# Seven block products instead of eight for the last product of attention and a bilinear FFN

## The chip, the cores and the metric

The kernel runs on one core of a Trainium2 chip. The metric is the time of one execution on the device in microseconds, the median of several runs. The profile is that of one execution, recorded on the chip. PE is the matmul engine, PEld its weight loads, DVE the vector engine, ACT the scalar engine, POOL GpSimd, SP the engine whose queue issues the transfers.

## The reference

```python
# attention over 32 memory slots: batch 8, 8 heads, 576 tokens, head_dim 64
a = softmax(phi, axis=2)                       # over tokens
k_m = einsum('bhsm,bhsd->bhmd', a, k); v_m = einsum('bhsm,bhsd->bhmd', a, v)
attn = softmax(q @ k_m.T / 8, axis=-1)         # 576 tokens x 32 slots
x = attn @ v_m                                 # heads side by side: 4608 tokens x 512
# bilinear FFN
g = (x @ w1) * (x @ w2)                        # 4608 x 1024
out = (g @ w3) @ w_out                         # 4608 x 512
```

The kernel uses that products may be bracketed otherwise: with M = v_m times w1 (or w2), (x @ w1) is attn @ M, and with W = w3 @ w_out (1024 x 512), computed once, out = g W.

## The kernel before, in words

All matmuls that matter take their operands in two pieces: a high part rounded to the fast fp32r format and a low part, the rest (`split`: ACT casts the high part, DVE subtracts to get the low one). A product is then three matmuls: high by high, low by high, high by low.

The work goes over 8 batches. A batch has 576 tokens in two halves n of 288. Its steps have names, and three lists at the top of the program (START, FIRST for batch 0, STEADY for the others) give the order in which they are written out. PE and SP run in exactly that order. The order within DVE, ACT and POOL is set by a scheduler when the kernel is built, which simulates a timeline; each engine then runs its list in order, one instruction after the other, and waits where an input isn't ready.

- START converts the float64 weights (step C: words picked apart on ACT and DVE), computes W in two halves (W), keeps it as pieces Wh, Wl (K), and prepares the attention of batch 0.
- A (`ab_unit`, 16 for each batch, one for each half n and each of eight f blocks of 128): two groups of six matmuls of 128x288, a = attn·M1 and b = attn·M2, into two PSUM banks. ACT copies a to SBUF, DVE multiplies it with b to g, and the split gives gh and gl.
- O (`out_part`, 16 for each batch: 2 halves n, 4 blocks o of 128 output features, 2 parts): 12 matmuls of 128x288, W's pieces by gh and gl, added up in one PSUM bank over both parts. ACT copies the result to osb and SP sends it out, 144 KB each, eight for a batch.
- The attention of the next batch lies between: `top`, `exp`, `norm` (softmax of phi, tile ph, among the A's), `turn`, `mem`, `blocks` (memories km, vm), and, among the O's, `sc` (scores), `se`, `sn` (softmax of the scores), `pr` (probabilities at, split to ah and al) and four M (`memory_weights`, split to mh and ml). `kv2`, `q2` and `phi2` are loads, issued by SP among its outputs.

PSUM has eight banks: a and b twice each, o twice, and a pair x.

Of the kernel before, what the change touches and what calls it, by code (L numbers as in the profile page):

```python
# [8 lines left out]
F32 = mybir.dt.float32  # L9
# [26 lines left out]
def memory_attention__then__bilinear_ffn_kernel(  # L36
# [39 lines left out]
    ps_o = ctx.enter_context(tc.tile_pool(name="ps_o", bufs=2, space=bass.MemoryType.PSUM))  # L76
    ps_x = ctx.enter_context(tc.tile_pool(name="ps_x", bufs=1, space=bass.MemoryType.PSUM))
# [73 lines left out]
    def attention(b):  # L151
# [22 lines left out]
        def turn(i):  # L174
            ps = psum_pair().rearrange("p k (c t x) -> p (k c) t x", c=2, t=NT)
# [40 lines left out]
        def blocks():  # L216
            ps = psum_pair()[:, 0, : NT * P]
# [7 lines left out]
        def scores(n, banks):  # L225
# [5 lines left out]
            ps = [x[:, :HALF] for x in banks()]  # L231
# [30 lines left out]
        def probs(n):  # L262
            if n == 0:
                v["at"] = att.tile([P, 2, S], F32, name="at", tag="ph")
                ah = att.tile([P, 2, S], F32R, name="ah", bufs=2)
                al = att.tile([P, 2, S], F32R, name="al", tag="al", bufs=2)
                ready["A", b] = (ah, al)
            ah, al = ready["A", b]
            nc.vector.transpose(out=v["at"][:, n], in_=v["s"][:, n].rearrange("p k m -> p (k m)"))
            split(ah[:, n], al[:, n], v["at"][:, n])  # L270

        steps = {"top": top, "exp": exp, "norm": norm, "mem": memories, "blocks": blocks}
        steps |= {f"turn{i}": lambda i=i: turn(i) for i in (0, 4)}
        for n in range(2):
            steps |= {f"sc{n}": lambda n=n: scores(n, pair), f"sc{n}p": lambda n=n: scores(n, banks_ab)}
# [7 lines left out]
    def memory_weights(b):  # L283
# [3 lines left out]
        def step(q, banks):  # L287
            one = None if banks else psum_pair()
            ps = banks() if banks else [one[:, t] for t in range(NT)]
            for g in range(NG):  # L290
                for t in range(NT):
                    d = slice((1 - t) * D, (2 - t) * D)
                    nc.tensor.matmul(  # L293
                        ps[t][g * M : (g + 1) * M],
# [7 lines left out]
            if banks:  # L302
                for t in range(NT):
                    split(mh[:, t], ml[:, t], ps[t].rearrange("p (w f) -> p w f", w=2))
            else:
                split(mh, ml, one.rearrange("p t (w f) -> p t w f", w=2))
# [20 lines left out]
    init = None  # L327
# [17 lines left out]
    def convert(i):  # L345
# [11 lines left out]
        if i < FIRST_LATE:  # L357
            u = init.tile([P, CW], I32, name="u", bufs=2)
# [190 lines left out]
```

## Time and profile before

| what | value |
|---|---|
| runs | 554.55, 555.44, 554.29 us; median 554.55 |
| profiled execution, span | 554.0 us |
| the median less the span | 0.55 us |
| a steady batch, from its first O to that of the next | 59.63 us |
| busy in one steady batch: PE, DVE, ACT, POOL | 59.63, 32.30, 25.13, 0.00 us |
| matmuls | 4696 |

The profile gives busy times by engine and groups of instructions by line, operation and tile; after the bar of a group stand the busy time, the mean duration in ns, and the idle time of the engine just before with what ended it. The chain is the work that ended last, followed backwards. In the timeline a row is start, duration, engine, line, operation, and in brackets the wait before it. Line numbers before and after the change differ: the split is L111/L112 before and L102/L103 after, and L495/L496 are the new splits of the block factors.

### The profile page before, as it was taken

The page shows a single profiled execution, that of the slowest core. Times are in us where ns is not written, and L with a number is a line of the kernel's source. Part 1 is how long each engine was busy: PE and PEld are TensorE (multiplying, and loading weights), DVE is VectorE, ACT ScalarE, POOL GpSimd, SP SyncE. Part 2 cuts the span into 40 slices and gives each one's busy share as a digit, 9 for nine tenths or more (in the row PEclk, how much of TensorE's full clock was granted, in tenths as well). Part 3 has the DMA queues.
Part 4 walks back from the last instruction along what each step waited for, and adds up shares of the span by engine and source line. Part 5 has one row for each costly group of instructions (what it writes and reads, how often), then busy time and mean ns, then how long its engine had stood idle before and what let it go on. Part 6 is the DMA issues. An engine that isn't in the chain of part 4 may idle for free.

```text
span 554.0 us, 11182 instructions
## 1 busy us (share of the span) xinstructions
PE 538.2 (97%) x4696; PEld 470.1 (85%) x4696; DVE 311.4 (56%) x599; ACT 253.7 (46%) x522; POOL 0.7 (0%) x6
## 2 busy tenths in 40 slices
PE   3999989999999999999999999999999999999997
PEld 1453458988999899989998899989998999899997
DVE  5887997637457624681558335762478155824500
ACT  5877784624544434452543444333544354424411
POOL 0000000000000000000000000000000000000000
PEclk9999999999999999999999999999999999999999
DMA  8999628008140511333043304050123200110011
GB/s 316 407 372 391 254 76 297 4 24 300 64 158 27 168 37 38 136 118 95 4 172 99 96 22 164 22 170 33 70 104 128 87 2 2 34 44 11 1 44 44
DMA packets 28819, 64.17 MB, mean 116 GB/s; under 512 B 2144, under 2 KB 10336, under 8 KB 28768
## 3 DMA queue, kind: packets, MB, share of 16 engines
q1 hardware_dynamic: 28768, 63.45, 32.7%
q8 instruction: 37, 0.61, 0.5%
q14 instruction: 14, 0.11, 0.1%
HBM read 54.00 MB, written 9.44 MB: 115 GB/s over the span
## 4 chain that ended last, share of the span: by engine, by line
PE 91%; DVE 4%; DMA 2%; ACT 1%; issue 1%; DVEq 0%; ACTq 0%
PE o L465 37%; PE a L440 18%; PE b L440 18%; PE x L194 3%; PE a L387 2%; PE b L387 2%; PE a L293 2%; PE x L293 2%; DMA raw<-in_w_out 1%; PE x L180 1%; PE b L293 1%; PE x L234 1%; DVE w L377 1%; DMA raw<-in_w3T 1%; DVE w L376 1%; PE o L387 1%
## 5 line engine op out<-in xcount | busy, mean ns | idle before, releaser
L465 PE MATMUL o<-gh,Wh 128*128 128x288 f32 x512 | 152.9, 299 | 0.0
L465 PE MATMUL o<-gl,Wh 128*128 128x288 f32 x512 | 151.1, 295 | 0.0
L465 PE MATMUL o<-gh,Wl 128*128 128x288 f32 x512 | 151.1, 295 | 0.0
L465 PEld LDWEIGHTS o<-gh,Wh 128*128 128x128 f32 x512 | 96.8, 189 | 11.9 <-issue 11.9
L451 DVE TENSOR_TENSOR gr<-b,a_sb 128x288 f32<-128x288 f32 x128 | 58.5, 457 | 84.2 <-PE b L440 80.9
L111 ACT CAST gh<-gr 128x288 fp32r<-128x288 f32 x128 | 55.4, 433 | 99.4 <-DVE gr L451 99.4
L465 PEld LDWEIGHTS o<-gl,Wh 128*128 128x128 f32 x512 | 96.3, 188 | 0.0
L465 PEld LDWEIGHTS o<-gh,Wl 128*128 128x128 f32 x512 | 96.2, 188 | 0.0
L112 DVE TENSOR_TENSOR gl<-gr,gh 128x288 fp32r<-128x288 f32 x128 | 58.5, 457 | 56.7 <-ACT gh L111 56.4
L440 PE MATMUL b<-ah,mh 128*128 128x288 f32 x256 | 75.6, 295 | 2.7 <-DVE Wl L112 2.7
L440 PE MATMUL a<-ah,mh 128*128 128x288 f32 x256 | 78.0, 305 | 0.0
L440 PE MATMUL a<-al,mh 128*128 128x288 f32 x256 | 75.9, 296 | 0.0
L440 PE MATMUL b<-al,mh 128*128 128x288 f32 x256 | 75.9, 296 | 0.0
L440 PE MATMUL b<-ah,ml 128*128 128x288 f32 x256 | 75.9, 296 | 0.0
L440 PE MATMUL a<-ah,ml 128*128 128x288 f32 x256 | 75.8, 296 | 0.0
L470 ACT COPY osb<-o 128x288 f32<-128x288 f32 x64 | 25.3, 395 | 82.8 <-PE o L465 71.5
L449 ACT COPY a_sb<-a 128x288 f32<-128x288 f32 x128 | 50.5, 394 | 8.0 <-PE a L440 7.4
L440 PEld LDWEIGHTS a<-ah,mh 128*128 128x128 f32 x256 | 48.4, 189 | 4.2 <-issue 2.0
L440 PEld LDWEIGHTS b<-ah,mh 128*128 128x128 f32 x256 | 48.4, 189 | 3.0 <-DVE Wl L112 3.0
L440 PEld LDWEIGHTS b<-ah,ml 128*128 128x128 f32 x256 | 48.5, 189 | 0.0
L440 PEld LDWEIGHTS a<-ah,ml 128*128 128x128 f32 x256 | 48.5, 189 | 0.0
L440 PEld LDWEIGHTS b<-al,mh 128*128 128x128 f32 x256 | 48.4, 189 | 0.0
(89 smaller groups left out, 649.1 us busy)
## 6 DMA issues: line engine op xcount, KB each, us to landing
kv<-in_kv SPq DMA_DIRECT2D x16, 1024.0 KB, 7.8
q<-in_qT SPq DMA_DIRECT2D x8, 1152.0 KB, 6.0
outT<-osb SPq DMA_DIRECT2D x64, 144.0 KB, 1.8
raw<-in_w3T SPq DMA_DIRECT2D x7, 1024.0 KB, 11.9
ph<-in_phiT SPq DMA_DIRECT2D x8, 576.0 KB, 4.0
raw<-in_w SPq DMA_DIRECT2D x4, 1024.0 KB, 17.2
raw<-in_w_out SPq DMA_DIRECT2D x3, 1024.0 KB, 10.5
kv<-in_w SPq DMA_DIRECT2D x3, 1024.0 KB, 14.5
```

Source lines behind the costliest of these rows:

```text
L111: nc.scalar.copy(out=hi, in_=src)
L112: nc.vector.tensor_tensor(out=lo, in0=src, in1=hi.bitcast(F32), op=ALU.subtract)
L180: nc.tensor.transpose(ps[:, c, t], v["ph"][:, t, at : at + P], ident)
L194: nc.tensor.matmul(ps[h * M : (h + 1) * M, t, : 2 * D], lhsT=v["a"][:, i, t, h * M : (h + 1) * M], rhs=kvt[i][:, (4 * t + h) * 2 * D : (4 ...
L234: nc.tensor.matmul(ps[t][g * M : (g + 1) * M], lhsT=km[b % 2][t * D : (t + 1) * D, g], rhs=v["q"][t * D : (t + 1) * D, g, n * HALF : (n + ...
L293: nc.tensor.matmul(ps[t][g * M : (g + 1) * M], lhsT=vm[b % 2][d, g], rhs=w12_sb[q][d, :, g], start=True, stop=True,)
L387: nc.tensor.matmul(pw[r][i], lhsT=x[:, i * P : (i + 1) * P], rhs=wos[k // half][:, k % half], start=k == 0, stop=k == NF - 1,)
L440: nc.tensor.matmul(p, lhsT=x[:, t, w, fc : fc + P], rhs=y[:, n, t * HALF : (t + 1) * HALF], start=i == 0, stop=i == len(todo) - 1,)
L449: nc.scalar.copy(out=a_sb, in_=ps[0])
L451: nc.vector.tensor_tensor(out=gr, in0=ps[1], in1=a_sb, op=ALU.mult)
L465: nc.tensor.matmul(v["p"], lhsT=x[f // half][:, f % half, oc], rhs=y, start=f == 0 and i == 0, stop=f == NF - 1 and i == 2)
L470: nc.scalar.copy(out=osb, in_=v["p"])
```

## The change

The matrix W is cut in four blocks (f halves by feature halves), and g in four (token halves n by f halves): G00, G01 for half 0, G10, G11 for half 1. The eight block products of the four output blocks become seven, by Strassen's scheme in Winograd's form, with sums of blocks of g on one side and sums of blocks of W on the other. The products are called 1, 2, 6, 5, 7, 3, 4 in the order in which they are used, and their factors on g's side X1 = G00, X2 = G01, X6 = S2, X5 = the sum of G10 and G11, X7 = S3, X3 = S4, X4 = G11. Each product is 2 O's (two column parts j of 128) of 12 matmuls, so a batch has 14 O's.

- `ab_unit` writes g into a 128x1152 tile of its block (no split there), and POOL does the block sums: S3 (L478), the sum in place of G10 (L480), S2 (L481), each four times 128x288, and S4 once 128x1152 (L489).
- `factor` (steps X1 to X7) splits a whole block: ACT casts 128x1152 into sh (L495), DVE subtracts into sl (L496), two buffers of each.
- `out_part`: products 1, 6, 7, 4 add up in the pair of banks o, 2 alone and 5, 3 in the pair x. After 1, 6, 5 and 4 ACT copies the running sum to a tile c (128x576); after 2, 7 and 3 DVE adds the PSUM pair to a c (L540). Four outputs of 288 KB go out, after 2, 7, 3 and 4.
- `keep` makes four blocks of pieces of W from raw copies: ACT copies and casts, POOL subtracts.
- PSUM is four pairs of two banks: ab twice, o, x. An A takes one pair and a pair is free when both its banks have been read. Scores and M use pairs of ab.
- The order lists change with it. ah and al have one buffer instead of two. In STEADY the load of ph stood with eight O's behind it and stands now behind the output of product 7, with three O's behind it.

```diff
-O sc0 sc1p Mp O se0 O se1 O q2 sn0 O pr0 O sn1 O pr1 M Mp Mp O phi2 O O O O O O O O
+O sc0p sc1p X6 O O se0 O X5 M M O se1 O X7 q2 sn0 O pr0 O sn1 X3 O pr1 M M O O X4 phi2 O O O
...
-        gr = big.tile([P, HALF], F32, name="gr", bufs=2)
-        nc.vector.tensor_tensor(out=gr, in0=ps[1], in1=a_sb, op=ALU.mult)
-        gh = big.tile([P, HALF], F32R, name=f"gh{n}{f}")
-        gl = big.tile([P, HALF], F32R, name=f"gl{n}{f}")
-        split(gh, gl, gr)
-        g[n, f] = (gh, gl)
...
+        nc.vector.tensor_tensor(out=G[n, f // half][:, k], in0=both[:, 1, :HALF], in1=a_sb, op=ALU.mult)
+        G["done"].add((n, f))
+        if (1 - n, f) in G["done"]:
+            sub = nc.gpsimd.tensor_tensor
+            top, low = G[0, 0][:, k], G[1, 0][:, k]
+            if f < half:
+                sub(out=G["S3"][:, k], in0=top, in1=low, op=ALU.subtract)
+            else:
+                sub(out=low, in0=low, in1=G[1, 1][:, k], op=ALU.add)
+                G["S2"].append(lambda: sub(out=top, in0=low, in1=top, op=ALU.subtract))
+
+    def factor(i, G):
+
+        if i == 6:
+            for f in G["S2"]:
+                f()
+            x = G[0, 1]
+            G["S4"] = lambda: nc.gpsimd.tensor_tensor(out=x, in0=x, in1=G[0, 0], op=ALU.subtract)
+        if i == 3:
+            G["S4"]()
+        src = {1: G[0, 0], 2: G[0, 1], 6: G[0, 0], 5: G[1, 0], 7: G["S3"], 3: G[0, 1], 4: G[1, 1]}[i]
+        hi = big.tile([P, half, HALF], F32R, name="sh", tag="sh", bufs=2)
+        lo = big.tile([P, half, HALF], F32R, name="sl", tag="sl", bufs=2)
+        in_turn("hi", nc.scalar.copy(out=hi, in_=src))
+        in_turn("lo", nc.vector.tensor_tensor(out=lo, in0=src, in1=hi.bitcast(F32), op=ALU.subtract))
+        G["X", i] = (hi, lo)
...
+        s, oc = weights[i]
+        oc = slice(oc * OH + j * P, oc * OH + (j + 1) * P)
+        hi, lo = G["X", i]
+        for k in range(half):
+            for m, (x, y) in enumerate(((Wh, hi), (Wl, hi), (Wh, lo))):
                 nc.tensor.matmul(
+                    ps[:, j, :HALF],
+                    lhsT=x[s][:, k, oc],
+                    rhs=y[:, k],
...
+        if i in (1, 6, 5, 4):
+            c = G["C", i] = const.tile([P, 2, HALF], F32, name="c", tag=f"c{n_c[0] % 4}")
+            n_c[0] += 1
+            nc.scalar.copy(out=c, in_=ps)
+        if i in (2, 7, 3):
+            c = G["C", {2: 1, 7: 5, 3: 6}[i]]
+            nc.vector.tensor_tensor(out=c, in0=ps, in1=c, op=ALU.add)
+        if i in (2, 7, 3, 4):
+            n, oh = {2: (0, 0), 3: (0, 1), 4: (1, 0), 7: (1, 1)}[i]
+            at = b * S + n * HALF
+            dst = outT[oh * OH : (oh + 1) * OH, at : at + HALF].rearrange("(j p) s -> p j s", j=2)
+            nc.sync.dma_start(out=dst, in_=c)
```

How the instructions stand, in rows of line, operation, out<-in and size. First DVE in the O phase of a steady batch, from the sums of the score softmax on. Before:

```order
L257 TENSOR_REDUCE ss_1914<-s_sb 128x18
L258 TENSOR_SCALAR ss_1875<-ss_1875 128x18
L258 TENSOR_SCALAR ss_1914<-ss_1914 128x18
L259 RECIPROCAL ss_1875<-ss_1875 128x18
L259 RECIPROCAL ss_1914<-ss_1914 128x18
L260 TENSOR_TENSOR s_sb<-s_sb,ss_1875 128x576
L260 TENSOR_TENSOR s_sb<-s_sb,ss_1914 128x576
L269 STREAM_TRANSPOSE at<-s_sb 128x576 x2
L112 TENSOR_TENSOR al<-at,ah 128x576 x2
```

And DVE in the same place in the change (g_1285 is the tile of G10, g_1283 that of G00, s_1287 is S3):

```order
L496 TENSOR_TENSOR sl<-g_1283,sh 128x1152
L249 TENSOR_REDUCE ss_1794<-s_sb 128x18
L249 TENSOR_REDUCE ss_1832<-s_sb 128x18
L540 TENSOR_TENSOR c<-x,c 128x576
...
L496 TENSOR_TENSOR sl<-g_1285,sh 128x1152
...
L103 TENSOR_TENSOR ml_1742<-ab,mh_1741 128x1024
...
L103 TENSOR_TENSOR ml_1755<-ab,mh_1754 128x1024
L252 TENSOR_TENSOR s_sb<-s_sb,ss_1832 128x576
L261 STREAM_TRANSPOSE at<-s_sb 128x576 x2
L496 TENSOR_TENSOR sl<-s_1287,sh 128x1152
L103 TENSOR_TENSOR al<-at,ah 128x576 x2
```

X6's and X5's subtractions, the addition of product 2 and two of the ml stand now among the softmax rows, and X7's (s_1287) stands behind both transposes.

Next DVE at the end of a steady batch and the start of the next, in the change:

```order
L540 TENSOR_TENSOR c<-o,c 128x576
L496 TENSOR_TENSOR sl<-g_1286,sh 128x1152
L540 TENSOR_TENSOR c<-x,c 128x576
L149 TENSOR_REDUCE mx<-ph 128x2
L160 TENSOR_SCALAR sm<-sm 128x2
L161 RECIPROCAL sm<-sm 128x2
L472 TENSOR_TENSOR g_1956<-ab,a_sb 128x288
```

Before, the maximum of ph stood behind the last ml and ahead of the first multiplication too; the additions c<-o,c (product 7) and c<-x,c (product 3) and X4's subtraction (g_1286) are new, and the load of ph is issued by SP behind the output that the first of them fills.

Last ACT around the first A's, where the last weights are converted and the probabilities of batch 0 are split. Before:

```order
L252 ACTIVATE s_sb<-s_sb 128x576
L111 CAST mh_435<-x 128x1024
L373 ACTIVATE w_2_83<-kv_388 128x1024
L373 ACTIVATE w_3_84<-q 128x1024
L111 CAST ah<-at 128x576
L374 ACTIVATE al<-kv_376 128x1024
L111 CAST Wh_474<-o 128x512 x2
```

And in the change:

```order
L361 ACTIVATE w_2_80<-kv_393 128x1024
L361 ACTIVATE w_3_81<-q 128x1024
L362 ACTIVATE ul<-q 128x1024
L361 ACTIVATE w_3_81<-kv_553 128x1024
L102 CAST ah<-at 128x576
L408 COPY raw_489<-ab 128x512 x2
L408 COPY raw_756<-o 128x512 x2
L389 CAST Wh_483<-raw_489 128x512 x2
L389 CAST Wh_483<-raw_756 128x512
```

Two more conversion rows stand ahead of the first ah, the last of them of the tile kv_553 that is loaded last, and raw copies stand ahead of the casts of W.

More of the change, by code (lines that the diff above doesn't have):

```diff
@@ L214, in memories, with blocks @@
                 )
[L216 to L217 removed]
+        def blocks(bank):
+            ps = bank()[:, 0, : NT * P]
             for t in range(NT):
@@ L223, in blocks, with scores @@
                 nc.vector.tensor_copy(out=vm[b % 2][vo : vo + D], in_=p4[vo : vo + D, t])
-        def scores(n, banks):
+        def scores(n, bank):
             if n == 0:
@@ L230, in scores @@
                 v["s"] = s_sb[:, : NT * S].rearrange("p (n k m) -> p n k m", n=2, m=M)
-            ps = [x[:, :HALF] for x in banks()]
+            both = bank()
+            ps = [both[:, t, :HALF] for t in range(NT)]
             for g in range(NG):
@@ L270, in probs @@
             split(ah[:, n], al[:, n], v["at"][:, n])
[L272 to L275, printed above, removed]
+        steps = {"top": top, "exp": exp, "norm": norm}
+        for x, bank in (("", pair_x), ("p", pair_ab)):
+            steps |= {f"turn{i}{x}": lambda i=i, bank=bank: turn(i, bank) for i in (0, 4)}
+            steps |= {f"mem{x}": lambda bank=bank: memories(bank), f"blocks{x}": lambda bank=bank: blocks(bank)}
+            steps |= {f"sc{n}{x}": lambda n=n, bank=bank: scores(n, bank) for n in range(2)}
         for name, f in (("se", soft_exp), ("sn", soft_norm), ("pr", probs)):
@@ L285, in memory_weights, with step @@
         ms = ready["M", b] = []
-        def step(q, banks):
-            one = None if banks else psum_pair()
-            ps = banks() if banks else [one[:, t] for t in range(NT)]
+        def step(q, bank):
+            ps = bank()
             for g in range(NG):
@@ L301, in step @@
             ml = const.tile([P, NT, 2, FQ], F32R, name=f"ml{q}", tag=f"m{m_tags[2 * q + 1]}")
[L302 to L306, printed above, removed]
+            split(mh, ml, ps.rearrange("p t (w f) -> p t w f", w=2))
             ms.append((mh, ml))
-        return [lambda banks=None, q=q: step(q, banks) for q in range(NQ)]
+        return [lambda bank, q=q: step(q, bank) for q in range(NQ)]
     def rows(w, k, n):
@@ L424, in memory_attention__then__bilinear_ffn_kernel, with ab_unit @@
                 steps[what]()
-    big = ctx.enter_context(tc.tile_pool(name="big", bufs=1))
-    def ab_unit(b, n, f, g):
+    last = len(START) - START[::-1].index("C")
+    with tc.tile_pool(name="init", bufs=1) as init:
+        for i in range(BUFS):
+            fetch(i)
+        start(START[:last])
+    big = ctx.enter_context(tc.tile_pool(name="big", bufs=1, reuse_waits="tile"))
+    start(START[last:])
+    def ab_unit(b, n, f, G):
         ah, al = ready["A", b]
@@ L432, in ab_unit @@
         fc = f * P % FQ
-        ps = []
-        for w, name in enumerate("ab"):
-            p = psum(ps_ab, name)[:, :HALF]
+        both = pair_ab()
+        for w in range(2):
             todo = []
```

160 lines of the change are left out of this document (96 added, 64 removed).

## The prediction

> **What bounds the kernel now.** I read the page's busy shares first, then the chain that ended last, then a table of stretches.
>
> ```profile
> PE 538.2 (97%) x4696; PEld 470.1 (85%) x4696; DVE 311.4 (56%) x599; ACT 253.7 (46%) x522; POOL 0.7 (0%) x6
> PE 91%; DVE 4%; DMA 2%; ACT 1%; issue 1%; DVEq 0%; ACTq 0%
> ```
>
> PE is busy for 97% of the span and 91% of the chain, but a busy share says nothing of where spare time lies. The table of stretches (span, then busy time of PE, PEld, DVE, ACT, POOL; clock; DMA share; GB/s) does, for one steady batch (start of one O phase to the next) and for the last O phase:
>
> ```profile
> 230.93:290.56 59.63, 59.63 (x574) 55.60 (x573) 32.30 (x66) 25.13 (x59) 0.00 (x0) 1.00 0.27 90
> 525.39:554.00 28.61, 25.46 (x192) 25.22 (x191) 0.92 (x2) 3.63 (x9) 0.00 (x0) 1.00 0.13 43
> ```
>
> In a steady batch PE has no gap in 59.63 us, at full clock. A matmul taken away is therefore time taken away, and any PE wait that appears is time added. The price of a matmul comes from the last O phase in the chain (start, us, what); the 295 to 299 ns that groups show are modelled ends which overlap.
>
> ```profile
> 108.59 1.59 PE o L465 x12
> ...
> 244.22 1.02 PE x L293 x16
> 246.96 14.52 PE o L465 x108
> ...
> 525.39 25.47 PE o L465 x192
> ```
>
> 25.47 / 192 = 0.1327 us for one matmul, 12 × 0.1327 = 1.59 us for one O.
>
> **1. Matmuls removed.** 14 O's instead of 16 in a batch, 24 matmuls fewer: 24 × 0.1327 × 8 = **-25.4 us**, all of it on the path.
>
> **2. The seventh product's low factor (X7).** The splits that stood in the A phase (one gh and gl for each A) become one cast and one subtraction of 128x1152 for each product, and four of the seven now run in the O phase, in DVE's queue among the next batch's softmax. What DVE did there before, and when:
>
> ```profile
> 230.77 0.29 PE L465 MATMUL o<-gh,Wh 128*128 128x288 f32 x1
> 233.28 0.85 DVE L243 STREAM_TRANSPOSE s_sb<-x 128x288 f32<-128x288 f32 x2 [0.82 <-PE x L234]
> 235.59 0.72 DVE L251 TENSOR_TENSOR s_sb<-s_sb,st 128x576 f32<-128x576 f32 x1
> 236.22 0.74 DVE L250 TENSOR_REDUCE st<-s_sb 128x18 f32<-128x576 f32 x1
> 241.91 1.43 DVE L269 STREAM_TRANSPOSE at<-s_sb 128x576 f32<-128x576 f32 x2
> 243.43 1.43 DVE L112 TENSOR_TENSOR al<-at,ah 128x576 fp32r<-128x576 f32 x2
> 253.62 1.35 DVE L158 TENSOR_REDUCE mx<-ph 128x2 f32<-128x1152 f32 x1 [3.61 <-DMA ph<-in_phiT]
> 263.18 0.46 DVE L451 TENSOR_TENSOR gr<-b,a_sb 128x288 f32<-128x288 f32 x1 [6.09 <-PE b L440]
> ```
>
> T is the first matmul of the O phase, 230.77. From T+2.5 the first four rows of DVE run back to back, and the two "at" transposes end at 243.34, T+12.6. DVE takes rows in order, and in the change X7's subtraction stands behind those transposes. Prices by size:
>
> ```profile
> L112 DVE TENSOR_TENSOR gl<-gr,gh 128x288 fp32r<-128x288 f32 x128 | 58.5, 457 | 56.7 <-ACT gh L111 56.4
> L112 DVE TENSOR_TENSOR al<-at,ah 128x576 fp32r<-128x576 f32 x16 | 11.5, 755 | 0.6
> L112 DVE TENSOR_TENSOR ml<-x,mh 128x1024 fp32r<-128x1024 f32 x11 | 13.5, 1225 | 9.2 <-ACT mh L111 9.2
> L111 ACT CAST gh<-gr 128x288 fp32r<-128x288 f32 x128 | 55.4, 433 | 99.4 <-DVE gr L451 99.4
> L111 ACT CAST ah<-at 128x576 fp32r<-128x576 f32 x16 | 10.7, 675 | 22.3 <-DVE at L269 22.3
> ```
>
> The step from 288 to 576 elements is 298 ns, so 1152 cost 755 + 2 × 298 = 1351 ns on DVE, and 675 + 2 × 242 = 1159 ns on ACT. Rows that follow each other on DVE start some 0.09 us sooner than their durations add up to (235.59 to 236.22 is 0.63 for a row of 0.72), so each is taken at 0.09 less, except the last. Now ahead of X7's subtraction and not there before: those of X6 and X5 (2 × 1.27), the addition after product 2 (128x576, taken as the 755 row: 0.66), and two ml of 128x1024 (2 × 1.14) where there was one in two halves of 0.6 (+1.1). T+12.6 + 2.5 + 0.7 + 1.1 + 1.35 = T+18.2. PE comes to the third matmul of product 7's first O, the first to read the low factor, after 8 O's (12.7), two scores (about 1.2 with their joints), two M (1.9 for both; the chain has 1.02 for one) and two matmuls (0.26): T+16.0. **It waits 2.2 us.** The cover is those 16 us; no other work of PE stands ahead. What is late next is X3's subtraction, one O later; it follows "al" on DVE by then in time. In six steady batches 6 × 2.2 = **+13.2**, in batch 0, whose queue is alike, **+2.5**. Bounds: if DVE's starts keep no order of mine and X7 slips ahead, 0; if ACT's casts hold DVE up by one cast, 3.4 each.
>
> Before product 6 the block sums on POOL have to be done. POOL computes nothing in the rows of before but these:
>
> ```profile
> masks.py:199 POOL TENSOR_SCALAR_AFFINE_SELECT ident<-ident 128x128 f32<-128x128 f32 x1 | 0.3, 292 | 0.1
> L536 POOL MEMSET const-bfloat16-1.0<- 128x1 bf16 x1 | 0.1, 102 | 0.0
> ```
>
> Estimates from them: in proportion to 128 elements in 292 ns, 288 cost 0.66 us and 1152 cost 2.6; at DVE's rate 0.46 and 1.35. I take the POOL row's. Then S2's last piece is there by about T+3.7, the cast and subtraction of X6 need 2.5 more, DVE's queue comes to it by T+7.9, and PE asks for it at T+9.7 (4 O's, the scores, two M); S4 of 2.6 us has until product 3. So the sums cost **nothing** at either bound: the 32 us of O phase hide them. Twice that price (1.3 a piece) would still reach X6 in time. For splits in the A phase (X1, X2) DVE has room, since its 128 gl rows of 0.46 us are gone.
>
> **3. The next batch's ph.** Its load is issued by SP, in order, behind the outputs. Before:
>
> ```profile
> 249.68 0.39 SPq L119 DMA_DIRECT2D ph<-in_phiT  x1
> ph<-in_phiT SPq DMA_DIRECT2D x8, 576.0 KB, 4.0
> L164 ACT ACTIVATE ph<-ph,mx 128x576 f32<-128x576 f32 x16 | 12.3, 770 | 18.7 <-DVE mx L158 18.7
> ```
>
> It went out at T+18.9, and the first multiplication of the next A's came at 263.18, after DVE had idled 6.09 us: well hidden. Now it stands behind the output of product 7, whose addition runs at about T+25 (12 O's and the stall), so it goes out at T+25.5, lands 4.0 later, and the maximum (1.35) and two exponentials (0.77 each, behind the copy of product 4 on ACT), then two small rows, come ahead of A's first multiplication in DVE's queue: T+33.2 to 33.7. A's third unit needs the pair of banks that this multiplication frees at T+32.7. I take **0.8 us in each of six batches, +4.8**; the bounds are 0 (it lands 1 us sooner) and 1.5.
>
> **4. Batch 0 and the start-up.** Rows of ACT, SP, DVE and PE around the first A's:
>
> ```profile
> 70.43 0.67 ACT L111 CAST ah<-at 128x576 fp32r<-128x576 f32 x1 [2.55 <-DVE at L269]
> 78.96 1.13 ACT L373 ACTIVATE w<-kv 128x1024 f32<-128x1024 f32 x1 [0.20 <-DMA kv<-in_w]
> 73.30 0.54 SPq L343 DMA_DIRECT2D kv<-in_w  x1
> 98.41 1.34 DVE L158 TENSOR_REDUCE mx<-ph 128x2 f32<-128x1152 f32 x1
> 75.13 0.40 PE L440 MATMUL a<-ah,mh 128*128 128x288 f32 x1
> 80.51 0.40 PE L440 MATMUL b<-ah,mh 128*128 128x288 f32 x1 [2.73 <-DVE Wl L112]
> 81.54 0.44 PE L440 MATMUL a<-al,mh 128*128 128x288 f32 x1
> 81.78 0.44 PE L440 MATMUL a<-ah,ml 128*128 128x288 f32 x1
> ```
>
> A conversion that waits for a load (issue to landing about 5.5 us, 73.30 to 78.8) now stands on ACT ahead of the first "ah", so that the second matmul of the first A starts near 77.8 instead of 75.4; behind it ACT now copies four products raw and casts both these and their sums where it had one cast for each, and the third A starts near 84.2 instead of 81.4. Then ph is asked for about 1 us later and X1's split and the maximum stand ahead of a multiplication. I carry **+5.3** to the first O; 3 if only the first wait stays, 8 if the W pieces on POOL (11264 elements a partition, 25 us in proportion to its row) hold ACT's casts up. In batch 0 the memories' blocks are followed by the scores with no O between, **+1.2** for DVE's four small copies.
>
> **5. The end.** The last matmul is followed by a copy and an output, now twice as large:
>
> ```profile
> 550.93 0.40 ACT L470 COPY osb<-o 128x288 f32<-128x288 f32 x1 [2.49 <-PE o L465]
> outT<-osb SPq DMA_DIRECT2D x64, 144.0 KB, 1.8
> ```
>
> +0.24 for the copy (433 to 675 ns is that step) and about +0.35 for twice the bytes (ph's 576 KB take 2.2 us more than 144): **+0.6**.
>
> **The sum** against the span of 554.0: -25.4 + 13.2 + 2.5 + 4.8 + 5.3 + 1.2 + 0.6 = +2.2, 556.2. The median of the runs, 554.55, lies 0.55 above the span; with it 556.8, and I say **557**. A steady batch is about as long as before: 59.63 - 3.18 + 2.2 + 0.8 = 59.45.
>
> **Rivals.**
>
> R1, POOL stops DVE. S4 (2.6 us, about T+3.7 to T+6.2) lies over DVE's first softmax subtraction, due at 235.59, T+4.8. If an instruction of DVE that reads two SBUF tiles stands until POOL's is over, the whole queue ahead of X7 moves by 1.4 us: 7 × 1.4, and about 1 us at X6 or X3 of the last batch: 557 + 11 = **568**. Against it: POOL's column is 0.00 in every steady stretch, so no run here shows either answer. That rule is in the Trainium skill, page "SBUF — State Buffer", section "Who interferes with whom": a DVE instruction with two SBUF inputs contends with a GpSimd instruction that reads SBUF, and the later one blocks fully.
>
> R2, X7 is not late. If DVE has the subtraction by T+16.0, 2.2 us sooner than I add up (rows that need less than I took, or a PE that comes later), the stalls of part 2 go and the change gains: 557 - 15.7 = **541**. For it: DVE is busy 32.30 of 59.63 us. Against it: the rows ahead stand in one queue and ran back to back before.
>
> R3, the waits cost PE its clock. After the gap of 2.73 us before 80.51, matmuls went 0.24 us apart (81.54 to 81.78) for some 2.5 us, about 1.1 us lost. If each wait of 2.2 us does it too, 7 × 1.1 and one at the start-up: **566**. For it: 2.2 us is close to 2.73. Against it: it is shorter, and the steady row, with its short joints at scores and M, has a clock of 1.00, so no row shows where between the two it turns.
>
> **How the numbers follow.** Forecast 0.40 (its own range 552 to 563: stalls of 1.5 to 3 us at X7), R1 0.30, R2 0.20, R3 0.10. About 0.2%, 1.1 us, is what a measurement can tell here. Faster: R2 and 0.04 of the forecast's low end, 0.24; same: 0.10 of the forecast, which lies just above; slower: the rest, 0.66. Half of R2 below 540 and the upper parts of R1 and R3 above 571 are left out, so the range is 540 to 571.
>
> **What would show it.** A PE wait of about 2 us for DVE's L496 at product 7's third matmul in batches 0 to 6, and none at the others (part 2); a DVE queue with no gaps ahead of it. A PE wait under 1.5 us at the third A of batches 1 to 6, ended by DVE's multiplication behind the maximum (part 3). The first O some 5 us later than 108.59 bears out part 4. R1 shows as a softmax subtraction of over 2 us on DVE while POOL runs L489; R2 as a PE with no gap in the O phase; R3 as a granted clock under 1.00 there. I am wrong at the root if PE waits for POOL (L481, L489) or for a bank.

## The result: 7% slower

The changed kernel takes 594.92 us (median of 592.76 to 595.85) against 555.00 for the kernel before (554.29 to 556.27), a ratio of 1.0705 [1.0676, 1.0733]. The forecast was 557, with a range of 540 to 571: the side came as forecast, the size did not. The profiled execution has a span of 593.8 us, 39.8 more than before.

Busy shares, and the granted clock in 40 slices, from the page of the changed kernel:

```profile
PE 540.2 (91%) x4504; PEld 452.1 (76%) x4504; DVE 354.0 (60%) x522; ACT 269.9 (45%) x413; POOL 134.0 (23%) x142
PEclk9998988999999989997999899999999799989999
PE 53%; DVE 27%; ACT 7%; DMA 6%; issue 4%; POOL 3%; SPq 0%; ACTq 0%; DVEq 0%; POOLq 0%
L523 PE MATMUL o<-sl,Wh 128*128 128x288 f32 x256 | 79.9, 312 | 21.9 <-DVE sl L496 21.9
```

PE does 192 matmuls fewer and yet is not busy for less time (540.2 against 538.2). Two things are new: 27% of the chain is DVE's (4% before), and the clock has dips. The last row shows one of the places where PE waits: 21.9 us in all ahead of the first matmul that reads a low factor.

The table of stretches (span, then busy time of PE, PEld, DVE, ACT, POOL; clock; DMA share; GB/s) for the start-up, one steady batch and the last O phase of the changed kernel:

```profile
0.00:122.59 122.59, 100.31 (x517) 59.11 (x518) 81.59 (x116) 80.69 (x107) 41.71 (x46) 0.96 0.65 239
378.61:442.06 63.45, 59.70 (x549) 52.53 (x549) 37.64 (x57) 26.22 (x44) 12.35 (x13) 0.97 0.26 85
566.00:593.80 27.80, 22.44 (x168) 21.97 (x166) 12.00 (x10) 8.94 (x11) 4.30 (x3) 1.00 0.12 43
```

Where the 39.8 us come from, by the starts of the batches (first O of each), with 3.18 us (24 matmuls) taken off what each batch took before:

| stretch | before, less 3.18 a batch | after | lost |
|---|---|---|---|
| to the first O | 108.59 | 122.59 | 14.0 |
| batch 0 | 59.53 | 65.53 | 6.0 |
| five steady batches | 5 x 56.45 | 318.27 | 36.0 (7.2 each) |
| the batch ahead of the last O phase | 52.76 | 59.61 | 6.8 |
| last O phase | 25.43 | 27.80 | 2.4 |
| all, less 25.4 for the matmuls | | | 65.2 - 25.4 = 39.8 |

Inside the steady batch of the second row the 7.0 us lost are: a PE wait for X7's low factor 3.06; the pair of M behind it 3.53 us long instead of 1.88, +1.65; the scores 1.48 instead of 1.13, +0.35; the first five A's, from the first to the last of them, +0.86; and about 1 us in short joints. Its O phase, PE's waits first and then DVE and POOL (timeline of the changed kernel: start, duration, engine, line, what, and in brackets the wait before; T, its first matmul, is 378.45):

```profile
398.65 0.41 PE L523 MATMUL o<-sl,Wh 128*128 128x288 f32 x1 [3.06 <-DVE sl L496]
415.66 0.40 PE L462 MATMUL ab<-ah,mh 128*128 128x288 f32 x1 [0.57 <-DVE g L472]
...
383.26 2.78 DVE L243 TENSOR_TENSOR s_sb<-s_sb,st 128x576 f32<-128x576 f32 x1
386.74 0.76 DVE L243 TENSOR_TENSOR s_sb<-s_sb,st 128x576 f32<-128x576 f32 x1
...
395.92 1.43 DVE L261 STREAM_TRANSPOSE at<-s_sb 128x576 f32<-128x576 f32 x2
397.28 1.32 DVE L496 TENSOR_TENSOR sl<-s,sh 128x1152 fp32r<-128x1152 f32 x1
...
382.75 2.68 POOL L489 TENSOR_TENSOR g<-g,g 128x1152 f32<-128x1152 f32 x1
```

The softmax subtraction that took 0.72 before takes 2.78 here, and it lies under POOL's S4, which starts 0.51 us ahead of it and ends at 385.43. The same instruction on the other half, 0.7 us later with POOL idle, takes 0.76. Two us later than it would be, DVE comes through its queue to X7, and PE waits for it. What the wait does to PE is in the table of stretches around it (the clock is the column behind POOL):

```profile
394.00:398.00 4.00, 1.59 (x13) 1.36 (x11) 4.00 (x6) 1.27 (x3) 0.00 (x0) 1.00 0.58 219
398.00:402.00 4.00, 3.35 (x34) 1.93 (x42) 3.20 (x4) 1.65 (x3) 0.00 (x0) 0.77 0.00 0
402.00:406.00 4.00, 4.00 (x41) 2.40 (x26) 2.27 (x2) 2.56 (x3) 0.00 (x0) 0.80 0.01 4
```

0.23 and 0.20 of two times 4 us are 1.7 us, the length by which the pair of M has grown. In two of the six batches (64.68 and 64.33 us long) the clock stayed at half for some 6 us behind the same wait. So the theory that the experiments had to test: **one POOL row stops a DVE row for 2.0 us (R1), the wait at X7 grows to a length behind which PE loses its clock (R3), and each steady batch pays both, 3.5 us in this one.** The rival: X7 is late because DVE's queue is too full, whatever POOL does, and S4 is a bystander. Apart from both stands the start-up, with its own 14.0.

### The profile page after: what moved, and what is told of

It reads as the page before. It is cut to its first block, busy times and chain, and to the rows that moved or that the text cites. A ratio compares the mean times of both kernels' runs of the same rounds, so it can differ in the third digit from the quotient of the medians.

```text
span 593.8 us, 10668 instructions
## 1 busy us (share of the span) xinstructions
PE 540.2 (91%) x4504; PEld 452.1 (76%) x4504; DVE 354.0 (60%) x522; ACT 269.9 (45%) x413; POOL 134.0 (23%) x142
## 3 DMA queue, kind: packets, MB, share of 16 engines
q1 hardware_dynamic: 28256, 63.45, 30.6%
## 4 chain that ended last, share of the span: by engine, by line
PE 53%; DVE 27%; ACT 7%; DMA 6%; issue 4%; POOL 3%; SPq 0%; ACTq 0%; DVEq 0%; POOLq 0%
PE ab L462 29%; PE o L523 7%; PE ab L375 5%; DVE sl L496 5%; DMA ph<-in_phiT 4%; DVE ml L103 4%; DVE s_sb L243 3%; PE ab L285 3%; DVE s_sb L235 2%; PE x L185 2%; DVE st L242 2%; DVE ss L249 2%; ACT ph L155 2%; POOL Wl L390 2%; PE x L523 2%
## 5 line engine op out<-in xcount | busy, mean ns | idle before, releaser
L462 PE MATMUL ab<-ah,mh 128*128 128x288 f32 x512 | 156.0, 305 | 12.4 <-DVE g L472 11.8
L462 PE MATMUL ab<-al,mh 128*128 128x288 f32 x512 | 152.5, 298 | 3.3 <-DVE al L103 3.3
L462 PE MATMUL ab<-ah,ml 128*128 128x288 f32 x512 | 152.2, 297 | 0.0
L462 PEld LDWEIGHTS ab<-ah,mh 128*128 128x128 f32 x512 | 97.5, 190 | 19.9 <-DVE g L472 16.4
L462 PEld LDWEIGHTS ab<-al,mh 128*128 128x128 f32 x512 | 97.5, 190 | 3.5 <-DVE al L103 3.5
L523 PE MATMUL o<-sl,Wh 128*128 128x288 f32 x256 | 79.9, 312 | 21.9 <-DVE sl L496 21.9
L462 PEld LDWEIGHTS ab<-ah,ml 128*128 128x128 f32 x512 | 97.6, 191 | 0.0
L478 POOL TENSOR_TENSOR s<-g,g 128x288 f32<-128x288 f32 x32 | 25.8, 805 | 289.1 <-DVE g L472 289.1
L496 DVE TENSOR_TENSOR sl<-g,sh 128x1152 fp32r<-128x1152 f32 x48 | 67.9, 1415 | 28.4 <-ACT sh L495 28.4
L523 PE MATMUL o<-sh,Wh 128*128 128x288 f32 x256 | 79.3, 310 | 0.0
L523 PE MATMUL o<-sh,Wl 128*128 128x288 f32 x256 | 77.4, 302 | 0.0
L495 ACT CAST sh<-g 128x1152 fp32r<-128x1152 f32 x48 | 55.5, 1156 | 42.8 <-PE o L523 28.5
L523 PEld LDWEIGHTS o<-sh,Wh 128*128 128x128 f32 x256 | 50.0, 195 | 17.1 <-issue 12.1
```

The lines of the kernel that those rows point to most:

```text
L462: nc.tensor.matmul(both[:, w, :HALF], lhsT=x[:, t, w, fc : fc + P], rhs=y[:, n, t * HALF : (t + 1) * HALF], start=i == 0, stop=i == len(to ...
L478: sub(out=G["S3"][:, k], in0=top, in1=low, op=ALU.subtract)
L495: in_turn("hi", nc.scalar.copy(out=hi, in_=src))
L496: in_turn("lo", nc.vector.tensor_tensor(out=lo, in0=src, in1=hi.bitcast(F32), op=ALU.subtract))
L523: nc.tensor.matmul(ps[:, j, :HALF], lhsT=x[s][:, k, oc], rhs=y[:, k], start=i in (1, 2, 5) and k == 0 and m == 0, stop=k == half - 1 and m ...
```

## Experiments on the steady batch

**S4 left out** (e1_no_s4). Product 3 takes G01 in the place of S4, so S4's block sum is not computed; everything else stands.

```diff
-        if i == 3:
-            G["S4"]()
```

> S4 is left out: product 3 takes G01 itself, so the output is another one; POOL has no 128x1152 row any more, all else stands. Theory (POOL stops DVE): the first softmax subtraction, 2.7 us in a steady batch of the changed kernel, is back at 0.75, so X7's low factor comes 2.0 us sooner and PE's wait for it falls from 3.1 to about 1.1 us; if the slow clock behind that wait goes too, another 1.7 us a batch. 594.9 less 7 x 2.0, and less 1.5 in the last batch, is about 579 with the slow clock and about 568 without. Rival (the subtraction is long for a reason of its own, such as its operands or PSUM): it stays at 2.7 us and the time within 2 us of 594.9.

Measured: 570.44 us, ratio 1.0272 [1.0256, 1.0288]; 24.5 us fewer than the change, for eight POOL rows of 2.7 us, for none of which PE shows a wait. The group of the first softmax subtraction (busy us, mean ns):

```profile
L243 DVE TENSOR_TENSOR s_sb<-s_sb,st 128x576 f32<-128x576 f32 x16 | 11.8, 740 | 0.2
```

In the changed kernel some six of its sixteen rows are stretched:

```profile
L243 DVE TENSOR_TENSOR s_sb<-s_sb,st 128x576 f32<-128x576 f32 x16 | 24.2, 1515 | 0.2
```

PE at product 7 without S4 (timeline):

```profile
385.24 0.40 PE L521 MATMUL o<-sl,Wh 128*128 128x288 f32 x1 [1.25 <-DVE sl L494]
```

The stretch behind that wait and a whole steady batch without S4:

```profile
385.30:389.30 4.00, 4.00 (x47) 2.45 (x48) 2.78 (x4) 2.29 (x4) 0.00 (x0) 1.00 0.00 0
367.27:427.44 60.17, 57.79 (x549) 52.30 (x549) 35.43 (x57) 26.00 (x44) 9.66 (x12) 1.00 0.27 90
```

The wait falls from 3.06 to 1.25, and the clock behind it stays at 1.00, so both halves of the 3.5 us go together. But S4 is also work taken away; so:

**S4 kept, and put elsewhere** (e5_s4_in_A). From batch 1 on S2 and S4 are computed piece by piece among the A's, and X2, which reads the tile that S4 overwrites, is split in four pieces there. POOL does the same arithmetic as in the change.

```diff
+        if b and n == 0 and f >= half:
+            piece(k, G)                      # cast and subtraction of X2's piece k
...
-                G["S2"].append(lambda: sub(out=top, in0=low, in1=top, op=ALU.subtract))
+                S2 = lambda: sub(out=top, in0=low, in1=top, op=ALU.subtract)
+                if b:
+                    S2()
+                    x = G[0, 1][:, k]
+                    sub(out=x, in0=x, in1=top, op=ALU.subtract)
```

> S4 is kept, but from batch 1 on X2 is split in four pieces of 128x288 as its blocks of g become ready, and POOL forms S2 and S4 piece by piece among the A's; batch 0 is as it was. Theory (it is S4's place over the softmax that costs, not S4): only one piece of 0.8 us is left near the first softmax subtraction, which falls from 2.7 to under 1.6 us; the wait at product 7 falls from 3.1 to 1.3 to 2 us, the slow clock behind it goes, and the time is 569 to 578, near the run without S4 (570.4). Rival (POOL's work stops DVE wherever it stands): the same microseconds return among the A's as waits for g, 585 or more.

Measured: 569.04 us, 1.0233 [1.0210, 1.0256], as fast as without S4. L243 means 736 ns, the wait at X7 is 1.01, the scores are back at 1.13 (in the change their second pair of banks waits for a multiplication that stands on DVE behind X2's subtraction of a whole block). So it is S4's place, not its amount, that costs about 25 us (of the 26 gained here some 2 are the scores). Among the A's DVE's rows are mostly multiplications of a PSUM and an SBUF tile, and their mean did not move (454 ns here, 455 in the change, 457 before). The pieces of X2, which read two SBUF tiles, are longer there too (724 ns on the mean of 28, where a split of this size took 457 before), but PE shows no wait for them.

**X7 ahead in DVE's queue** (e2_x7_sooner). S4 stays where it was, the stretched subtraction too; X7's subtraction is put ahead of the second softmax multiplication and the transposes.

```diff
             nc.vector.tensor_tensor(out=sv, in0=sv, in1=ss.broadcast_to([P, NBLK, M]), op=ALU.mult)
+            if n == 1:  # this one is scheduled behind X7's subtraction, and so are both transposes
+                behind(ins, "X7")
```

> X7's subtraction stands on DVE ahead of the second softmax multiplication and of both transposes of at, behind the second ml; nothing else is changed. Theory (X7 waits in DVE's queue): it begins at about T+16.7 instead of T+18.8, PE waits 1.0 us instead of 3.1, which is 2.1 us in each of 7 batches, about 580; if a wait of 1 us leaves the clock alone, another 1.7 us a batch, about 568. Rival (the buffers bound it: X7's cast can begin only when product 6 has given its buffer back, T+13.5, and X7 is late whatever its place): the wait stays above 2.5 us and the time above 590.

Measured: 577.18 us, 1.0394 [1.0377, 1.0411]. L251's mean is still 1509 ns, as the theory had it, but the wait is 1.05 (timeline):

```profile
388.44 0.40 PE L534 MATMUL o<-sl,Wh 128*128 128x288 f32 x1 [1.05 <-DVE sl L507]
```

and the clock stays at 1.00 (stretches, a steady batch):

```profile
370.40:431.23 60.83, 58.31 (x549) 52.40 (x549) 37.39 (x57) 26.04 (x44) 12.32 (x13) 1.00 0.26 89
```

So the wait can be taken away from its other end too: a stretched DVE row costs only if someone waits. It gains less than e1, and misses the 568 that was expected with the clock kept: DVE's 2 us are still spent, so the transposes are later. This batch is 60.8 us, the five steady ones of e1 are 59.6 to 60.2; about half of the difference lies in the A's, where the wait at the third A grew from 0.57 to 1.12, and half in the O phase, where it was not traced.

**The clock by itself** (e9_m_ahead). The second pair of M is written ahead of product 7's first O, so PE has 2 us of work where it waited. S4, the stretched row and DVE's order stay. (The list of batch 0 is changed alike.)

```diff
-O sc0p sc1p X6 O O se0 O X5 M M O se1 O X7 q2 sn0 O pr0 O sn1 X3 O pr1 M M O O X4 phi2 O O O
+O sc0p sc1p X6 O O se0 O X5 M M O se1 O X7 q2 sn0 O pr0 O sn1 X3 M M O pr1 O O X4 phi2 O O O
```

> Only PE's order is changed: the second pair of M stands ahead of product 7's first O instead of behind it, so that PE works where it waited; DVE's order in the steady batches is as in the change, X7's low factor no sooner. Theory (the length of the wait costs the clock): the wait for the low factor falls from 3.1 to about 1.2 us, the granted clock stays at 1.00 behind it, and a steady batch loses 1.9 us of wait and 1.7 us of slow matmuls less: 594.9 less about 7 x 3.3, 572 (568 to 576). Rival (the clock falls in this place for another reason than the wait's length): the wait falls alike but the clock still drops below 0.85 in the four microseconds behind it, 580 to 586.

Measured: 579.46 us, 1.0420 [1.0389, 1.0450]. PE in the timeline, at product 7 and at the third A:

```profile
329.70 0.40 PE L523 MATMUL o<-sl,Wh 128*128 128x288 f32 x1 [0.97 <-DVE sl L496]
...
344.43 0.40 PE L462 MATMUL ab<-ah,mh 128*128 128x288 f32 x1 [1.58 <-DVE g L472]
```

The stretches around the first of them:

```profile
328.00:332.00 4.00, 3.03 (x27) 2.60 (x20) 4.00 (x5) 4.00 (x6) 0.00 (x0) 1.00 0.01 2
332.00:336.00 4.00, 4.00 (x32) 4.00 (x31) 4.00 (x5) 1.70 (x2) 0.00 (x0) 1.00 0.00 0
```

The wait fell by the 2.1 us that the M's fill, and with it the clock's loss went, with all that stretches DVE still there: the two prices of the chain (stretch, clock) are apart. The time missed what was expected. The wait at the third A says why: PE reaches the next A's sooner, ph does not, and the wait at the third A grows from 0.57 to 1.58. A batch is 61.16 us where 0.57 would have made it 60.15.

**ph sooner** (e3_ph_sooner). Its load is written right behind `pr1`, ahead of the output of product 7, and its maximum is put behind X4's subtraction on DVE. (The list of batch 0 is changed alike.)

```diff
-O ... sn1 X3 O pr1 M M O O X4 phi2 O O O
+O ... sn1 X3 O pr1 phi2 M M O O X4 O O O
```

> The load of ph stands in SP's order behind the second split of the probabilities, ahead of the output of product 7, and its maximum on DVE right behind X4's subtraction. Theory (ph late): the load goes out at about T+21.5 instead of T+28.9, the exponentials are done before the first A, and the wait of 0.6 us at the third A with its joint goes: 0.8 us in each of 6 batches, about 590. Rival (the load is still late, or the earlier maximum makes X4's or product 3's addition late): 594 to 600.

Measured: 591.12 us, 1.0646 [1.0611, 1.0682]; its interval still touches that of the change, so the gain of about 3.8 us is weakly resolved. A batch is 62.44 instead of 63.45, and the wait at the third A is gone. This agrees with the 0.86 of the ledger.

**All three** (e6_steady): S4 among the A's, X7 ahead, ph sooner.

> The three edits of the steady batch together: S2 and S4 in pieces among the A's, X7's subtraction sooner on DVE, the load of ph sooner. Theory: the three waits are separate and add up; no PE wait for the low factor over 0.5 us, none at the third A, a steady batch of 57 to 58 us (59.63 less 3.18, and about 1 us of joints): 594.9 less 7 x 6.0, about 553 (550 to 560). Rival (one of them covers for another, a new wait takes their place, product 6 or 5 the likeliest): a steady batch of 59 us or more, 562 to 570.

Measured: 553.49 us, 0.9958 [0.9943, 0.9974], 0.4% below the kernel before. A steady batch in the table of stretches:

```profile
299.36:356.63 57.27, 57.27 (x550) 52.39 (x549) 36.71 (x61) 26.56 (x46) 12.91 (x17) 1.00 0.28 94
```

PE has no gap and the full clock; POOL is busy as long as in the change. 57.27 less 56.45 leaves 0.8 us a batch unexplained by any wait: the joints. So of the 7.0 us of the batch shown first, 3.5 were S4's place (1.8 of wait, by e1, and 1.65 of clock), the rest of X7's wait 1.25, ph 0.9, the scores 0.35 and the joints 0.8; 0.2 are left over.

## Experiments on the start-up

Where the 14.0 us are: the first A starts at 78.57 instead of 75.13 (+3.4), and from there to the first O it takes 44.02 instead of 33.46 (+10.6). In that stretch PE waits 10.9 us against 2.73 before (timeline of the changed kernel, each wait of over 0.4 us behind the first A's first matmul):

```profile
82.27 0.40 PE L462 MATMUL ab<-al,mh 128*128 128x288 f32 x1 [3.30 <-DVE al L103]
88.65 0.40 PE L462 MATMUL ab<-ah,mh 128*128 128x288 f32 x1 [1.54 <-DVE g L472]
94.97 0.40 PE L462 MATMUL ab<-ah,mh 128*128 128x288 f32 x1 [1.65 <-DVE g L472]
100.36 0.61 PE L462 MATMUL ab<-ah,mh 128*128 128x288 f32 x1 [3.54 <-DVE g L472]
109.12 0.40 PE L462 MATMUL ab<-ah,mh 128*128 128x288 f32 x1 [0.86 <-DVE g L472]
```

Behind them stand, in the same kernel, a conversion on ACT that waits for the last weights, DVE rows stretched while POOL is busy without a gap (1.28 for an "al" of 0.75, 2.31 for an L365), and casts on ACT that wait for POOL's W sums:

```profile
76.78 1.17 ACT L361 ACTIVATE w<-kv 128x1024 f32<-128x1024 f32 x1 [4.15 <-DMA kv<-in_w]
77.86 0.66 ACT L102 CAST ah<-at 128x576 fp32r<-128x576 f32 x1
80.94 1.28 DVE L103 TENSOR_TENSOR al<-at,ah 128x576 fp32r<-128x576 f32 x1
85.92 2.31 DVE L365 CUSTOM_DVE_ANT_0 w<-w,ua 128x2048 uint16<-128x2048 uint16 x1
93.51 0.62 ACT L389 CAST Wh<-raw 128x512 fp32r<-128x512 f32 x1 [2.29 <-POOL raw L412]
```

The stretch from the first A to the first O, and two pieces of it:

```profile
78.57:122.59 44.02, 33.13 (x234) 29.98 (x235) 24.58 (x32) 23.94 (x44) 32.33 (x32) 0.92 0.28 95
78.57:90.00 11.43, 6.59 (x34) 6.15 (x35) 11.40 (x12) 9.80 (x16) 10.85 (x9) 0.85 0.00 0
...
98.00:106.00 8.00, 5.64 (x33) 5.64 (x34) 2.86 (x6) 3.28 (x8) 8.00 (x11) 0.79 0.66 225
```

Behind the waits of 3.30 and 3.54 the clock is below 1.00. ACT has the copies of the A's behind such a cast, DVE's multiplication stands behind the copy, and PE needs the pair of banks that it frees.

**The casts of W's sums on POOL** (e4_w_casts), the start-up's first suspect by itself.

```diff
-        nc.scalar.copy(out=Wh[s][:, i], in_=src)
+        (nc.gpsimd.tensor_copy if s > 1 else nc.scalar.copy)(out=Wh[s][:, i], in_=src)
```

> The high pieces of the two W blocks that are sums (slots 2 and 3) are cast on POOL, not on ACT; POOL has 8 rows more. Theory (ACT stands in line behind POOL): the copies of a, which stood behind those casts, are no longer held; of the waits of PE for g in the start-up (1.54, 1.65, 3.54, 0.86 us) the second and third go, and the first O comes 4 to 6 us sooner than 122.6: about 590. Rival (the start-up is late because POOL slows DVE's own rows, which the longer POOL chain makes worse): the first O at 122 or later and the time at 594 to 600.

Measured: 594.73 us, 1.0719 [1.0685, 1.0754], no change, and that theory missed. The waits behind the casts did go, but the first O came only 2.3 us sooner, and batch 0 gave it back (69.0 us instead of 65.5). A wait of 3.11 took their place; DVE had a row ahead of its multiplications that waited for ph, whose load stands behind kv and q in SP's order, and then a row of two elements that POOL stretched:

```profile
105.22 1.35 DVE L149 TENSOR_REDUCE mx<-ph 128x2 f32<-128x1152 f32 x1 [4.61 <-DMA ph<-in_phiT]
108.26 2.31 DVE L160 TENSOR_SCALAR sm<-sm 128x2 f32<-128x2 f32 x1 [1.33 <-ACT ph L155]
```

**The start-up rearranged** (e7_start): ah's cast ahead of the last conversions on ACT, ph loaded ahead of kv and q, W's sums cast behind the tenth A's copy (the new step S). The steady batches stay those of the change.

```diff
-A C A C A N A A C A C A kv1 A A A q1 N K10 phi1 top A X1 K11 A exp A A norm turn0 A X2 A
+A C A C A N A A C A C A phi1 kv1 A K10 K11 A A S q1 N top A X1 A exp A A norm turn0 A X2 A
```

> Start-up alone: ACT splits the probabilities of batch 0 ahead of the last conversions, ph is loaded ahead of kv and q, and the casts of the W blocks that are sums come in one piece behind the a copy of the tenth A; the steady batches are as in the change. Theory (three queue orders make the 14 us: ACT behind a load, ACT behind POOL, ph behind other loads): the waits of 3.30, 1.65 and 3.54 us go, the first O comes at 110 to 114 instead of 122.6, and the time is 583 to 588. Rival (POOL's W chain bounds it: 26 us from the last product of W on): the first O at 119 or later, 591 or more.

Measured: 588.38 us, 1.0591 [1.0563, 1.0619], and a first O at 117.3: 5.3 us sooner, where 8.6 or more were looked for. The old waits went, and new ones came (timeline):

```profile
81.98 0.61 PE L478 MATMUL ab<-ah,mh 128*128 128x288 f32 x1 [4.27 <-ACT raw L419]
87.66 0.40 PE L478 MATMUL ab<-ah,mh 128*128 128x288 f32 x1 [2.53 <-DVE g L488]
```

and the clock fell behind the second of them (stretches):

```profile
88.00:90.00 2.00, 2.00 (x12) 2.00 (x10) 1.86 (x2) 2.00 (x6) 2.00 (x3) 0.58 0.63 256
```

ACT has the raw copies of W's banks, the conversions and the A's copies to do in these 15 us, and whatever is put first makes another wait.

**Start-up and steady batches together** (e8_all: e6 with e7).

> The steady edits and the start-up edits together. Theory: they are apart in time, so the gains add: the time of the run with the steady edits less what the run with the start-up edits gains on 594.9, 540 to 550, below the kernel before by 1 to 2%. Rival (the start-up is longer for the pieces that wait for each other, and the steady joints stay): 553 or more, no faster than the kernel before.

Measured: 549.53 us, 0.9896 [0.9877, 0.9915], first O at 117.76. Three more orders of the start-up on top of it, which move the same work in other ways: in the first (e10_all_2) the raw copies stand ahead of the conversions; in the second (e11_all_3) the conversions stand a pair behind the A's copies, and the W pieces of the second half all behind the ninth A; in the third (e12_all_4) the pieces that need no sum stand right behind the raw copies, and only the sums' casts among the seventh to tenth A's.

```diff
-A C A C A N A A C A C A phi1 kv1 A K10 K11 A A S q1 N top A X1 A exp A A norm turn0 A X2 A
+K10 K11 A C phi1 A C A A A C N A C A S A S kv1 A S A S q1 A N top A exp A X1 A norm turn0 A X2 A
```

> The kernel of the last run with its start-up ordered further: ACT copies the products of W raw ahead of the last conversions, the maximum of ph stands on DVE behind the multiplication of the tenth or eleventh A, and the casts of the W sums stand one pair behind each of four copies of a. Theory: the waits of 4.28, 2.60 and 1.94 us in the start-up go or halve, the first O comes at 110 to 114 instead of 117.8, and the time is 543 to 546. Rival (POOL's W chain, whose end frees X1's buffer, bounds the first O): the first O at 116 or later, 548 or more.

> The steady edits with another start-up: on ACT the conversions of the last weights stand one pair behind the copies of a of the first, second, fifth and sixth A, and every cast of W's second half stands behind the ninth A or later; the third and fourth M come later among the A's. Theory (the start-up of the change is lost in the order of ACT's queue): the first nine A's run without a wait over 1 us, the first O comes at 108 to 113, and the time is 540 to 546. Rival (POOL's W chain, now ending near 108, or the conversions themselves bound it): the first O at 116 or later, 548 or more.

> As the last run, but the pieces of W's third block (slot 1) are made right behind its raw copies and only the casts of the two blocks of sums stand behind the seventh to tenth A, so that POOL has work from the end of W on. Theory (POOL's W chain was the bound of the last run: it stood idle from 83 to 98 us and ended at 113): POOL ends at 100 to 104, X1's buffer is free before the last A, the wait of 2.7 us and that of 3.1 us at the first O go, the first O comes at 109 to 112, and the time is 543 to 547. Rival (ACT's and DVE's conversions, with their last load landing at 88, bound the A's): the first O at 114 or later and 549 or more.

Measured: 550.72 us (0.9914 [0.9900, 0.9928]) for e10, 551.57 (0.9929 [0.9913, 0.9945]) for e11, both missed. In e10 the A's copies came behind the conversions and PE waited 8.18 us at once, at 87.81; in e11 its rival was right: POOL was busy for 1.6 us of the 11 from 87 to 98, its last W pieces ended at 116.6, and PE waited 2.72 and 3.05 at the first O for the two pieces of X1, whose cast on ACT waits for a W piece on POOL. The third, e12, takes **546.10 us, 0.9844 [0.9817, 0.9870]**: 1.6% faster than the kernel before, 8.2% than the change, and the best of all. Its time came out as expected, its first O at 114.7 did not (109 to 112 was looked for); waits of 1.84, 2.05, 1.50 and 1.60 stay among the A's. The start-up and a steady batch of e12 in the table of stretches:

```profile
0.00:114.70 114.70, 95.92 (x517) 55.52 (x518) 83.35 (x116) 80.18 (x107) 42.24 (x46) 1.00 0.70 256
292.43:349.69 57.26, 57.26 (x550) 52.39 (x549) 36.91 (x61) 26.53 (x46) 12.91 (x17) 1.00 0.27 94
```

None of its waits among the A's is over 2.05 us, and the start-up's clock is 1.00 instead of 0.96.

## Why the prediction was wrong, by its own steps

- **Part 1, matmuls: right.** Where PE has no gap the batch is 57.26 us against 59.63, which is 24 matmuls (3.18) less 0.8 of joints.
- **Part 2, X7: right in mechanism and on DVE's side, 1.1 us off on PE's.** Without S4 PE has X7's low factor at T+18.1 (18.2 was predicted). In the change PE came at T+17.1 and not at T+16.0: the O's with their joints take 1.7 instead of 1.59 and the scores 1.48. So the wait is 2.2 less 1.1 for PE, plus 2.0 for the stretched row: 3.1. In batch 0 it was 2.06 (2.5 predicted). The sums cost PE no wait at X6 in a steady batch, as said; in the last batch they did. There S4 lies over X6's subtraction, which takes 2.75, and PE waits 1.49.
- **POOL's price: a fifth too low for 288 elements, right for 1152.** 805 and 2686 ns, where 0.66 and 2.6 us were taken from the proportion; the bound at DVE's rate (1.35) was far off.
- **Part 3, ph: right.** Issued at T+28.9 and not at 25.5, but the A's were later by as much; 4.4 us to land, a wait of 0.57 at the third A and +0.86 in the first five A's, where 0.8 was taken. In e3, without it, the A's of batches 1 to 6 are 5.2 us shorter in all, where 4.8 was taken; but the 5.2 are not even, 1.9 of them lie in batch 1.
- **Part 4, start-up: a term mis-sized by 8.7, 5.3 taken and 14.0 measured.** The first wait was seen (the conversion that waits for a load, 4.15 us on ACT), and 8 was the bound if POOL holds up ACT's casts. It left out that the rows of this stretch hold each other up at once: POOL is busy for 32.33 of the 44.02 us, stretches DVE's al and conversions, and is waited for by ACT; and two of the PE waits that follow cost clock too (0.85 and 0.79 in their stretches). How much each of these makes is not shown: e4 and e7 took single waits away, and others came. Batch 0's 1.2 was 0.5 at km; from its first O to that of batch 1 it lost 6.0 where 4.5 was taken (2.5, 1.2 and one 0.8 of ph), since ph's wait there was 1.67 us.
- **Part 5, the end: right in size,** from the start of the last matmul to the end 4.16 us instead of 3.45, +0.7 against 0.6. Its 0.35 for twice the bytes does not follow from its own rate, though: 2.2 us for 432 KB more is 0.73 for 144.
- **The step that failed is the price of the block sums in part 2, "nothing", with R1 and R3 put as rivals that exclude each other.** The sum asked whether POOL is done in time, and not what its rows do to DVE's meanwhile; that was left to R1, the slow clock to R3, and no case had both. Both were true, and R1 brings R3 on: the wait that the queue alone makes (1.25 us in e1) kept the clock in all six steady batches, and the 2.0 us that POOL adds on DVE bring it to 3.06, behind which the clock fell in all six of the change. R1 was priced at 1.4 us in each batch, by an S4 that was to end 0.8 us sooner than it did; it is 1.8 of wait and, with the clock, 3.5. Even R1's 11 and R3's 9 together would have made only 577. R1's own sign came as written: a subtraction of 2.78 under L489. R2 fell, since PE waited in all of batches 0 to 6, if by 1.25 us only where S4 was out.

By the rule that the prediction cited for R1 (the Trainium skill, "SBUF — State Buffer", "Who interferes with whom") the DVE row stands until POOL's is over; the trace agrees: POOL's row ends at 385.43, and the subtraction, which ended at 386.04, had 0.61 of its 0.74 us still to do. The page has it that reductions never contend on this chip and that a DVE row with at most one SBUF input does not, outside the modes that use both ports; here the reductions (747 ns) and the multiplication of a PSUM and an SBUF tile (455) were not stretched.

What the sum would have been with the measured terms: -25.4 for the matmuls, 14.0 start-up, 6.0 batch 0, 42.8 in six batches and 2.4 at the end, 593.8. Of the 37.6 us by which that exceeds the predicted span of 556.2, S4's place makes about 25 (e1, e5; the 1.49 of the last batch among them), the start-up 8.7 and batch 0 1.5, and some 2 are left. That so little is left is in part luck: the sum had nothing for the joints and the scores (0.8 and 0.35 a batch), and X7's own wait was 1.25 instead of 2.2.

## What to carry to other kernels

An engine that does nothing is not free to give work to: price what its work does to the rows of its neighbours while it runs, and put such work where those rows are of the kind that isn't held (here among the multiplications that read PSUM, not over the softmax). Add up the small delays that meet at one wait before judging whether the wait is harmless: here waits of up to 1.8 us among the products were paid for once, as time, and waits of 3.05 us in most cases twice, as time and as clock. And rivals that feed each other are no alternatives: give their joint case a price of its own.

## What the hardware showed that was not expected

- **A held row, both ways, whatever its size.** Beside L243 (0.74 alone, up to 2.78), a row of 128x2 elements took 2.31 us (L160, in the start-up of e4); it ended 0.02 us behind the last of four POOL rows that ran without a gap. POOL's own rows grew too in the start-up, where DVE was busy beside them: L390 of 512 elements took 1558 ns on the mean of twelve, with 1260 the shortest and 2263 the longest.
- **Where the clock turns: no sharp length.** In all kernels, behind PE waits of 0.9 to 1.8 us the clock stayed at 1.00 in the next 4 us. Of nine waits of 2.05 to 2.11 us five lost it. All four of 2.53 to 2.73 did, though two of them stood some 5 us behind a wait of 4.3. Of the 24 waits of 3.04 to 3.06 at X7 (the change, e3, e4, e7) 21 lost it and three did not. The same wait of 2.06 us in batch 0, in the changed kernel and in e1:

```profile
144.93 0.40 PE L523 MATMUL o<-sl,Wh 128*128 128x288 f32 x1 [2.06 <-DVE sl L496]
144.18 0.41 PE L521 MATMUL o<-sl,Wh 128*128 128x288 f32 x1 [2.06 <-DVE sl L494]
```

and the stretches behind them in the same order; the third row is the stretch behind a wait of 3.04 us at X7 in e4, where the clock stayed:

```profile
145.00:149.00 4.00, 4.00 (x47) 2.45 (x48) 3.59 (x6) 2.30 (x4) 0.00 (x0) 1.00 1.04 293
144.20:148.20 4.00, 4.00 (x34) 2.15 (x42) 3.33 (x5) 1.16 (x3) 0.00 (x0) 0.64 1.06 342
272.40:276.40 4.00, 4.00 (x47) 2.45 (x48) 2.78 (x4) 2.28 (x4) 0.00 (x0) 1.00 0.02 4
```

That e4 batch's O phase is 31.6 us long; with the clock lost behind a wait as long it is 32.9 to 34.5, so the clock's price alone was 1.3 to 2.9 us. A longer wait loses the clock more often, but its length does not decide alone, and what else does stays open here. The six lost at shorter waits, of 1.83 to 1.97 us, all stood at one place, the small products 44 us into the start-up, where the clock fell in six kernels of thirteen. The Trainium skill ("TensorE: Matmul & The Clock Gate", Part 1) has the clock fall after at least one idle window of about 3.4 us; most of the waits here that cost it were shorter than that, so where page and measurement differ the measurement decides.
- **0.8 us a batch at joints.** Even where no wait shows, a batch is 0.8 us longer than its matmuls by the price of before. Nothing was run to split it.
